# Differences of inputs moved from GpSimd to VectorE, and another order of the seven products, in a kernel of sparse attention and a gated feed-forward layer

## The chip, the cores and the metric

The kernel runs on one core of one Trainium2 chip. The metric is the device time of one execution in microseconds (us). Before the change the median of three runs is 895.81 us (894.02 to 897.63). The core has five engines that run side by side: TensorE (PE in the rows; PEld is its weight load), VectorE (DVE), ScalarE (ACT), GpSimd (POOL) and SyncE (SP), whose queue issues the DMAs.

## The reference

Eight batches of eight heads, 576 positions, 64 numbers per head. Heads 0 to 3 see the last 32 positions ("local"), heads 4 to 7 see the earlier positions with the same remainder modulo 32 ("strided"). The outputs of all heads of a position form a row x of 512 numbers; the 4608 rows then go through a feed-forward layer. All is fp32:

```python
scores = np.where(masks, q @ k.T / 8, -1e9)          # per head, mask local or strided
x = softmax(scores) @ v                              # heads side by side: 4608 x 512
h = x @ w_in                                         # 512 x 2048
g = h * (1.0 / (1.0 + np.exp(-1.702 * h)))
return g @ w_out                                     # 2048 x 512
```

## The kernel before

**Tiling.** The rows are nine groups of 512 tokens (`G`). The hidden dimension is 16 blocks of 128 (`NF`). An fp32 product is made of three products on TensorE of operands that are split in a high part (a cast on ScalarE, `high`, `split`, `high_x`, `halves`) and a low part (a subtraction, on VectorE or GpSimd): high by high, high by low, low by high. The gate is computed as (tanh(0.851 h) + 1) * h; the factor 0.5 is applied to the results.

**Attention units.** `_pairs()` lists units of attention, local and strided, in the order in which they are worked on; a unit fills a part of the x tiles of one or two groups. A unit goes through scores (PE), mask, scale and maximum (DVE, `maxima`), eight exps (ACT, `softmax`), a scaling by the inverse sums (POOL), 32x32 transposes (DVE, `transpose`, into the tile `pt_l` or `pt_s`), and the product with v (PE, `values`), whose result ACT and DVE copy into the x tiles. Units are spread over the feed-forward work of earlier groups; `TURNS` gives the step of the transposes for the first three groups.

**Plain groups.** Groups 0, 1 and 2 run as 48 steps (`steps`, loop `for s in range(2, len(steps))`): step s makes block f of the hidden layer (`ffn1`, 12 products into tile `h`), and two steps later its share of the result (`ffn2`, 12 products into the four banks `o`). During group 0 the weights are decoded and split. During group 2, `sum_up` makes for each of eight pairs of hidden blocks the sums of weights that the next stage needs: `add_up` on GpSimd (tiles `plain`, `summed`), `high_sums` on ACT, `low_sums` on DVE, and DMAs to DRAM. `SUMS` gives the steps.

**Pairs of groups.** The groups (3,4), (5,6), (7,8) are worked on two at a time (`DOUBLES`). The product with w_in for two groups by two hidden blocks is done by a scheme of Strassen and Winograd: seven products in place of eight. The operands of tokens are b11, b21 (first group, local and strided half), b12, b22 (second group) and the differences t1 = b12 - b11, t2 = b22 - t1, t3 = b22 - b12, t4 = b21 - t2 (`difference`), each with a high and a low part (`high_x`, `low_x`). The operands of weights a11, a12, a22 and the sums s1 to s4 stream from DRAM (`load_sum`). The partners are a11 with b11, s2 with t2, a12 with b21, s3 with t3, a22 with t4, s1 with t1, s4 with b22. In the trace the product of k is `ha` or `hs`, its operands `b11h`, `b11l`, `t2h`, `t2l` and so on.

A pair has eight *rounds* (`cycle`, c = 0 to 7), each with the seven products in the order of `BLOCKS`; after each product `fill(GAPS[i])` puts 4, 4, 4, 3, 3, 3, 3 products of the second layer (`o`) into PE's queue, from a list of generators (`filling`). VectorE and ScalarE combine the seven products into four hidden blocks in the tiles `spare` (s1, u2, v5, z) and `y`. Two blocks belong to the first group and are used at once. The two of the second group wait in DRAM (`gates`) until the *pass* that follows the eight rounds: 16 slots of 12 `o` products each, one hidden block per slot, loaded into `spare` and split by `halves` (ACT writes `gh`, DVE writes `gl`). In the last slots of the pass the operands of the next pair are prepared. In the tables of the engines below "opening" means the first round of a pair (c = 0).

**Order.** Each engine runs its own queue in the order in which the code issues the instructions (`InOrder` keeps it), so the places of calls in the loops set the order on every engine. Six PSUM banks are shared by the four `o`, the products of the rounds and `values`: a product of a round needs the bank of the product two before it, which is free once that one was read (by a DVE add, an ACT copy, or both).

**Tiles.** Results leave through tiles of the tag `st2` (four slots), which also holds the `y` tiles of the rounds; weights, x tiles, operands, streams and sums share 42 larger slots (`w_tile`).

## Time and profile before

| | |
|---|---|
| median of three runs | 895.81 us (894.02 to 897.63) |
| the profiled execution | 896.67 us, of which 894.9 us from the first instruction to the last |
| TensorE busy | 863.7 us (97%) |
| VectorE, ScalarE, GpSimd busy | 571.5, 426.4, 226.7 us |
| granted TensorE clock, mean | 0.992 of full speed |

Busy times overlap, since the engines run side by side. A row of the profile that shows "idle before" names the engine whose semaphore came last. All instructions have one line (L129), that of the class that keeps the order; they are told apart by the names of their tiles.

### The profile page before, as it was taken

The numbers are of one execution on the slowest core, as the hardware profiler recorded it, in microseconds if no ns is written. First come the engines' busy times: TensorE is split into PE (matmuls) and PEld (weight loads), VectorE is DVE, ScalarE is ACT, GpSimd is POOL, SyncE is SP. The second block draws the span as 40 slices with busy tenths as digits, with TensorE's granted clock in tenths as the row PEclk, the third lists the DMA queues.
The fourth block names the chain that finished last, engine by engine and source line by source line (L and its number), as shares of the span: only waits on it lengthen the run. The fifth ranks groups of instructions, "written<-read, shape, count | busy, mean of one in ns | idle before, by whom it ended". The sixth has DMA issues, their size and how long they took to land. (4 is left out here: it accounts for less than half of the span.)

```text
span 894.9 us, 15595 instructions
## 1 busy us (share of the span) xinstructions
PE 863.7 (97%) x5690; PEld 691.6 (77%) x5690; DVE 571.5 (64%) x988; ACT 426.4 (48%) x1224; POOL 226.7 (25%) x188
## 2 busy tenths in 40 slices
PE   8999999999999997999999989999999899999998
PEld 5787668888888875778887768788888688888886
DVE  4789977655676887666666686676653754444522
ACT  7798864344455455444535544553433423232421
POOL 4001001100354935232232051223220412222100
PEclk9999999999999999999999999999999999999999
DMA  9956225541263554656557525655545235454442
GB/s 282 326 228 223 100 74 177 172 162 54 79 211 117 183 166 153 208 190 191 187 183 242 177 80 159 212 175 158 161 149 196 71 112 183 146 171 146 143 124 71
DMA packets 75581, 146.40 MB, mean 164 GB/s; under 512 B 8240, under 2 KB 22960, under 8 KB 75504
## 3 DMA queue, kind: packets, MB, share of 16 engines
q1 hardware_dynamic: 75504, 145.40, 50.5%
q8 instruction: 45, 0.74, 0.3%
q14 instruction: 32, 0.26, 0.1%
HBM read 108.67 MB, written 36.70 MB: 162 GB/s over the span
## 5 line engine op out<-in xcount | busy, mean ns | idle before, releaser
L129 PE MATMUL o<-w,gh 128*128 128x512 f32 x1152 | 368.4, 396 | 0.0
L129 PEld LDWEIGHTS o<-w,gh 128*128 128x128 f32 x1152 | 216.8, 189 | 47.5 <-ACT gh L129 0.2
L129 PE MATMUL o<-w,gl 128*128 128x512 f32 x576 | 226.8, 394 | 8.0 <-DVE gl L129 8.0
L129 PEld LDWEIGHTS o<-w,gl 128*128 128x128 f32 x576 | 109.0, 189 | 33.5 <-DVE gl L129 11.1
L129 DVE SCALAR_TENSOR_TENSOR y<-tanh,y 128x512 f32<-128x512 f32 x96 | 66.5, 692 | 103.4 <-ACT tanh L129 103.4
L129 POOL TENSOR_TENSOR pr<-pr,rinv 128x432 f32<-128x432 f32 (+1 forms) x42 | 50.7, 1206 | 308.1 <-DVE rinv L129 308.1
L129 POOL TENSOR_TENSOR gl<-y,gh 128x512 fp32r<-128x512 f32 x45 | 58.1, 1291 | 226.7 <-ACT gh L129 226.7
L129 ACT ACTIVATE tanh<-y 128x512 f32<-128x512 f32 x96 | 60.7, 633 | 101.6 <-DVE y L129 95.0
L129 ACT ACTIVATE pr<-pr,nmax 128x54 f32<-128x54 f32 (+1 forms) x296 | 101.0, 346 | 0.0
L129 DVE TENSOR_TENSOR gl<-spare,gh 128x512 fp32r<-128x512 f32 x48 | 41.0, 855 | 62.2 <-ACT gh L129 61.0
L129 PE MATMUL h<-xl,w 128*128 128x512 f32 x288 | 75.9, 398 | 2.2 <-DVE w L129 0.9
L129 PE MATMUL h<-xs,w 128*128 128x512 f32 x288 | 75.2, 396 | 1.8 <-ACT xs L129 1.7
L129 ACT CAST gh<-spare 128x512 fp32r<-128x512 f32 x48 | 29.9, 622 | 79.7 <-PE o L129 79.5
L129 PEld LDWEIGHTS h<-xs,w 128*128 128x128 f32 x288 | 54.7, 191 | 14.0 <-ACT xs L129 2.1
L129 PEld LDWEIGHTS h<-xl,w 128*128 128x128 f32 x288 | 52.4, 188 | 16.6 <-DVE w L129 3.2
L129 ACT ACTIVATE g<-h 128x512 f32<-128x512 f32 x48 | 28.7, 597 | 69.8 <-PE h L129 46.0
L129 DVE STREAM_TRANSPOSE pt_l<-pr 32x256 f32<-32x256 f32 x128 | 55.6, 434 | 3.7 <-POOL pr L129 1.9
L129 DVE SCALAR_TENSOR_TENSOR g<-g,h 128x512 f32<-128x512 f32 x48 | 32.8, 684 | 39.0 <-ACT g L129 39.0
L129 ACT ACTIVATION_READ_ACCUMULATOR pr<-pr,nmax 128x1 f32 x296 | 56.4, 191 | 0.0
L129 DVE STREAM_TRANSPOSE pt_s<-pr 32x256 f32<-32x256 f32 x126 | 54.8, 435 | 2.3 <-POOL pr L129 0.5
L129 DVE TENSOR_TENSOR spare<-hs,spare 128x512 f32<-128x512 f32 x72 | 48.7, 677 | 2.1 <-PE hs L129 1.1
L129 ACT CAST gh<-g 128x512 fp32r<-128x512 f32 x48 | 29.7, 619 | 35.4 <-PE o L129 31.5
(130 smaller groups left out, 1258.3 us busy)
## 6 DMA issues: line engine op xcount, KB each, us to landing
stream<-s SPq DMA_DIRECT2D x96, 256.0 KB, 2.7
stream<-a SPq DMA_DIRECT2D x72, 256.0 KB, 2.7
gate<-y SPq DMA_DIRECT2D x48, 256.0 KB, 2.0
spare<-gate SPq DMA_DIRECT2D x48, 256.0 KB, 2.8
qk<-sqk SPq DMA_DIRECT2D x23, 452.0 KB, 4.3
qk<-lqk SPq DMA_DIRECT2D x18, 576.0 KB, 4.9
out<-out SPq DMA_DIRECT2D x36, 256.0 KB, 2.5
raw<-w_in SPq DMA_DIRECT2D x16, 512.0 KB, 7.7
```

The costliest lines, as they stand in the source:

```text
L129: ins = call(*args, **kw)
```

## The change

It has seven parts:

1. All differences of inputs and all low parts run on VectorE (`difference`, `low_x`), none on GpSimd. For the second and third pair they are spread over slots 1 to 15 of the pass before (they stood in slots 10 to 15), and the parts of t4 and b22 come in the opening.
2. In the opening the seven products come in the order `OPENING`: a11, a12, s1, s2, s3, a22, s4. v5 is made there by a copy of the product s1 and a later add of u2. For the first pair t1 is made in step 46; the others come in the opening, between its products.
3. `SUMS`: four of the eight sums of weights are made in group 1 (steps 17 to 23), four in group 2 (33 to 39).
4. `TURNS`: the units of groups 1 and 2 come one step later; in two of the windows the order of units is another one.
5. In step 16 the second layer's products come ahead of the first layer's.
6. The results of groups 2, 4, 6 and 8 go through large slots, two results to a tile.
7. In every round the tanh and the multiplication by it are issued apart, with another product's add between them; the transposes of a unit come in four portions instead of two, the exps in four portions of two.

```diff
-TURNS = ((5, 7, 9, 11, 13), (0, 2, 4, 6, 8, 10, 12, 14), (0, 2, 4, 6, 8, 10, 12))
+TURNS = ((5, 7, 9, 11, 13), (1, 3, 5, 7, 9, 11, 13, 15), (1, 3, 5, 7, 9, 11, 13))
+OPENING = ("a11", "a12", "s1", "s2", "s3", "a22", "s4")
+SUMS = (17, 19, 21, 23, 33, 35, 37, 39)
...
                     vector.transpose(out=pt[at, :, i], in_=pr[i, :, o])
-            yield
+                yield
...
-                    o = st2([P, DM], F32, f"out_{j}_{i}")
+                    if j < NN - 1 or j % 2:
+                        o = st2([P, DM], F32, f"out_{j}_{i}")
+                    else:
+                        if i % 2 == 0:
+                            two = w_tile([P, 2, DM], F32, f"out_{j}_{i}")
+                        o = two[:, i % 2]
...
-    SUMS = (0, 2, 4, 6, 8, 9, 11, 13)
...
-            at = s - (NN - 1) * NF - SUMS[c]
+            at = s - SUMS[c]
...
-        engine.tensor_tensor(out=x, in0=a, in1=b, op=ALU.subtract)
+        vector.tensor_tensor(out=x, in0=a, in1=b, op=ALU.subtract)
...
+    def convert(d, *ks):
+        for k in ks:
+            high_x(d, k)
+            low_x(d, k)
...
-        if s == -7:
-            high_x(0, "b21")
-            low_x(0, "b21", vector)
-        if s == -5:
-            high_x(0, "b11")
-            low_x(0, "b11", vector)
+        if s == -6:
+            convert(0, "b21")
+        if s == -4:
+            convert(0, "b11")
         if s == -2:
-            high_x(0, "b22")
-            low_x(0, "b22", vector)
+            difference(0, "t1")
+            convert(0, "t1")
...
-    def gate(x, y):
+    def curve(x):
         g = ffn.tile([P, G], F32, tag="g2", name="tanh", bufs=1)
         scalar.activation(g, x, AF.Tanh, scale=0.851)
-        vector.scalar_tensor_tensor(out=y, in0=g, scalar=1.0, in1=x, op0=ALU.add, op1=ALU.mult)
+        yield
+        vector.scalar_tensor_tensor(out=x, in0=g, scalar=1.0, in1=x, op0=ALU.add, op1=ALU.mult)
...
+        for i, k in enumerate(order):
+            t = ps[k] = bank(f"h{k}_{d}_{c}")
+            product(t, k)
...
+            if k == "s2":
+                add(u2, t, s1)
+                if not c:
+                    add(v5, v5, u2)
+            if k == "a12":
+                y[0] = st2([P, G], F32, f"y_{a}_{f}")
+                add(y[0], t, s1)
+                first_y = curve(y[0])
+                run(first_y, 1)
+            if k == "s3":
+                add(z, t, u2)
+                scalar.copy(out=s1, in_=t)
+                run(first_y)
+                halves((a, f), y[0], gpsimd)
...
+            if k == "s1":
+                if c:
+                    add(v5, t, u2)
+                else:
+                    scalar.copy(out=v5, in_=t)
...
+            start(i)
+            if i in (1, 2, 3, 4):
+                turned()
+            if i in (1, 2, 3, 4):
+                eased(1)
+            if i == 5:
+                eased(HU)
...
     for s in range(2, len(steps)):
+        if s == NF:
+            ffn2(s - LAG)
         ffn1(s)
...
-        if s >= LAG:
+        if s >= LAG and s != NF:
             ffn2(s - LAG)
...
-    difference(0, "t1", vector)
-    difference(0, "t2", vector)
-    difference(0, "t3", gpsimd)
+    difference(0, "t2")
     high_x(0, "t2")
-    low_x(0, "t2", vector)
-    high_x(0, "t3")
+    difference(0, "t3")
+    low_x(0, "t2")
...
         if i == 0:
             split(len(steps) - 1)
-            low_x(0, "t3", vector)
+            high_x(0, "t3")
+            difference(0, "t4")
         if i == 1:
-            difference(0, "t4", gpsimd)
-            high_x(0, "t1")
-            low_x(0, "t1", gpsimd)
+            low_x(0, "t3")
             high_x(0, "t4")
-            low_x(0, "t4", vector)
+        if i == 2:
+            low_x(0, "t4")
+            high_x(0, "b22")
+        if i == 3:
+            low_x(0, "b22")
...
-                    10: lambda: (high_x(d + 1, "b11"), low_x(d + 1, "b11", vector), difference(d + 1, "t1", gpsimd)),
...
+                    1: lambda: convert(d + 1, "b11"),
+                    2: lambda: convert(d + 1, "b21"),
+                    6: lambda: difference(d + 1, "t1"),
+                    7: lambda: convert(d + 1, "t1"),
+                    11: lambda: difference(d + 1, "t2"),
+                    12: lambda: convert(d + 1, "t2"),
+                    13: lambda: difference(d + 1, "t3"),
+                    14: lambda: convert(d + 1, "t3"),
+                    15: lambda: difference(d + 1, "t4"),
```

In the order of VectorE around the first opening, before. `xl` and `xs` are x tiles in which a difference is left, `t` holds t2, `gl_3834` is the low part of step 47's hidden block, `hs_0_0_3842` the product of s2 with t2, the second of the opening:

```order
L129 TENSOR_TENSOR xl_0_2834<-xl_0_3422,xl_0_2834 128x1024
L129 TENSOR_TENSOR t_0_3814<-xs_0_2433,xl_0_2834 128x1024
L129 TENSOR_TENSOR t2l<-t_0_3814,t2h 128x1024
L129 TENSOR_TENSOR gl_3834<-g_47_3787,gh_3833 128x512
L129 TENSOR_TENSOR t3l<-xl_0_3422,t3h 128x1024
L129 TENSOR_TENSOR spare_3751<-hs_0_0_3842,spare_3751 128x512
```

And after. `ha_0_0_3839` is the product of a12, now the second; `hs_0_0_3884` and `hs_0_0_3904` are those of s2 and s3, the fourth and the fifth:

```order
L131 TENSOR_TENSOR t_0_3811<-xs_0_2537,xl_0_2942 128x1024
L131 TENSOR_TENSOR xl_0_3500<-xs_0_2537,xl_0_3500 128x1024
L131 TENSOR_TENSOR t2l<-t_0_3811,t2h 128x1024
L131 TENSOR_TENSOR gl_3828<-g_47_3751,gh_3827 128x512
L131 TENSOR_TENSOR xs_0_1836<-xs_0_1836,t_0_3811 128x1024
L131 TENSOR_TENSOR y_0_3847<-ha_0_0_3839,spare_3725 128x512
L131 TENSOR_TENSOR t3l<-xl_0_3500,t3h 128x1024
L131 STREAM_TRANSPOSE pt_s<-pr_98 32x8x32
L131 TENSOR_TENSOR t4l<-xs_0_1836,t4h 128x1024
L131 STREAM_TRANSPOSE pt_s<-pr_98 32x8x32 x2
L131 TENSOR_TENSOR spare_3725<-hs_0_0_3884,spare_3725 128x512
L131 TENSOR_TENSOR spare_3726<-spare_3726,spare_3725 128x512
```

The difference t1 (first row before) has gone to step 46, t3 and t4 (second and fifth row after) have come from GpSimd, and between the read of a12 and that of s2 stand two low parts and three transposes.

In the order of VectorE in the pass of the first pair, slots 10 to 14, before. `gl_10` is the low part of hidden block 10 of the second group, which PE needs in the slot that follows; the low parts between are those of the second pair's operands:

```order
L129 TENSOR_TENSOR gl_10_5576<-spare_3751,gh_10_5575 128x512
L129 TENSOR_TENSOR b21l<-xs_0_2976,b21h 128x1024
L129 TENSOR_TENSOR gl_11_5597<-spare_3752,gh_11_5596 128x512
L129 TENSOR_TENSOR b22l<-xs_0_3973,b22h 128x1024
L129 TENSOR_TENSOR gl_12_5617<-spare_3752,gh_12_5616 128x512
L129 TENSOR_TENSOR t1l<-xl_0_4162,t1h 128x1024
```

And after, the same blocks:

```order
L131 TENSOR_TENSOR gl_10_5579<-spare_3725,gh_10_5578 128x512
L131 TENSOR_TENSOR t_1_5583<-xs_0_3973,xl_0_4161 128x1024
L131 TENSOR_TENSOR gl_11_5598<-spare_3726,gh_11_5597 128x512
L131 TENSOR_TENSOR t2l<-t_1_5583,t2h 128x1024
L131 TENSOR_TENSOR gl_12_5617<-spare_3726,gh_12_5616 128x512
L131 TENSOR_TENSOR xl_0_5036<-xs_0_3973,xl_0_5036 128x1024
```

There is still one operation on 1024 columns between two of these low parts; the differences, which ran on GpSimd beside them (tiles `xl`, `t`, `xs`), are now among them.

## Rows read from the trace of the kernel before

**Rows 1.** The page's slices: TensorE's busy share, tenths, 40 equal slices.

```profile
PE   8999999999999997999999989999999899999998
```

**Rows 2.** What TensorE waited for: us in total, times, longest us.

```profile
PE o L129 <- DVE gl L129: 8.0, 4, 3.1
...
PE hs L129 <- DVE spare L129: 2.6, 2, 1.4
...
PE h L129 <- ACT xs L129: 1.7, 1, 1.7
PE hs L129 <- ACT t2h L129: 1.5, 1, 1.5
PE a L129 <- DVE spare L129: 1.3, 5, 0.3
PE hs L129 <- DVE t2l L129: 1.0, 1, 1.0
...
PE hs L129 <- ACT spare L129: 0.8, 3, 0.3
PE ha L129 <- issue: 0.8, 1, 0.8
```

**Rows 3.** Two rows of TensorE's timeline in group 2: start, us, instruction [idle before].

```profile
314.46 0.96 PE L129 MATMUL a<-pt_s,v 118*64 118x108 f32 x16 [1.31 <-DVE pt_s L129]
...
328.72 0.92 PE L129 MATMUL a<-pt_l,v 96*64 96x64 f32 x24 [0.77 <-DVE pt_l L129]
```

**Rows 4.** Windows; after the five busy times: granted clock, DMA share, GB/s.

```profile
131.00:138.00 7.00, 6.64 (x38) 4.88 (x42) 5.19 (x11) 3.62 (x8) 0.91 (x1) 0.76 0.00 0
...
533.00:540.00 7.00, 6.67 (x29) 5.54 (x30) 6.20 (x7) 2.52 (x3) 0.00 (x0) 1.00 0.00 0
715.00:722.00 7.00, 6.69 (x22) 5.34 (x23) 5.64 (x7) 2.52 (x3) 0.00 (x0) 0.76 0.00 0
```

**Rows 5.** The timeline of VectorE and GpSimd in the first pair's pass.

```profile
527.10 3.42 DVE L129 TENSOR_TENSOR b22l<-xs,b22h 128x1024 fp32r<-128x1024 f32 x1
...
529.40 3.32 POOL L129 TENSOR_TENSOR xl<-xs,xl 128x1024 f32<-128x1024 f32 x1
...
530.44 2.83 DVE L129 TENSOR_TENSOR gl<-spare,gh 128x512 fp32r<-128x512 f32 x1
533.20 1.21 DVE L129 TENSOR_TENSOR t1l<-xl,t1h 128x1024 fp32r<-128x1024 f32 x1
...
534.33 0.68 DVE L129 TENSOR_TENSOR gl<-spare,gh 128x512 fp32r<-128x512 f32 x1
```

**Rows 6.** The timeline at both openings of the first two pairs.

```profile
338.43 1.17 DVE L129 TENSOR_TENSOR xl<-xl,xl 128x1024 f32<-128x1024 f32 x1
...
339.64 1.82 DVE L129 TENSOR_TENSOR t<-xs,xl 128x1024 f32<-128x1024 f32 x1
...
367.27 0.60 ACT L129 ACTIVATE out<-o 128x512 f32<-128x512 f32 x1 [4.51 <-DMA out<-out]
...
537.19 1.05 ACT L129 CAST t4h<-xs 128x1024 fp32r<-128x1024 f32 x1
...
542.90 1.77 DVE L129 STREAM_TRANSPOSE pt_l<-pr 32x256 f32<-32x256 f32 x4
```

**Rows 7.** A group of the page: ScalarE's exps, busy us, mean ns of one.

```profile
L129 ACT ACTIVATE pr<-pr,nmax 128x54 f32<-128x54 f32 (+1 forms) x296 | 101.0, 346 | 0.0
```

**Rows 8.** The chain that ended last, third pair's opening: start, us.

```profile
722.23 1.36 PE ha L129 x6
724.49 1.36 PE hs L129 x6
...
731.07 1.36 PE ha L129 x6
733.11 1.36 PE hs L129 x6
```

**Rows 9.** A window in group 2 with sums of weights in it; columns as in rows 4, busy times ahead.

```profile
280.00:300.00 20.00, 20.00 (x129) 16.07 (x128) 13.06 (x24) 11.85 (x43) 13.26 (x14) 1.00 0.39 128
```

More of the change, by code (lines that the diff above doesn't have):

```diff
@@ L527, in second @@
         gh, gl = gs.pop(g)
+        two = None
         for i in range(NT):
@@ L827, in cycle @@
         final = (d, c) == (len(DOUBLES) - 1, NF // 2 - 1)
-        def of(k):
-            ps = bank(f"h{k}_{d}_{c}")
-            product(ps, k)
-            if not final:
-                load_sum((c + 1) % (NF // 2), k)
-            return ps
+        after = p + 1 if p is not None and p + 1 < len(pairs) else None
+        order = BLOCKS if c else OPENING
+        ps, y = {}, {}
+        if p is not None:
+            turning[p] = transpose(p)
         def turned():
@@ L838, in turned @@
                 run(turning[p], 1)
-        if p is not None:
-            turning[p] = transpose(p)
-        after = p + 1 if p is not None and p + 1 < len(pairs) else None
-        ps = of("a11")
-        scalar.copy(out=s1, in_=ps)
-        start(0)
-        fill(gaps[0])
-        ps = of("s2")
-        add(u2, ps, s1)
-        turned()
-        start(1)
-        if after is not None:
-            run(soft[after], 2)
-        fill(gaps[1])
-        ps = of("a12")
-        y = st2([P, G], F32, f"y_{a}_{f}")
@@ L856, in cycle @@
-        add(y, ps, s1)
-        gate(y, y)
-        halves((a, f), y, gpsimd)
-        fill(gaps[2])
-        ps = of("s3")
-        add(z, ps, u2)
-        scalar.copy(out=s1, in_=ps)
-        turned()
-        if after is not None:
-            run(soft[after], 2)
-        fill(gaps[3])
-        ps = of("a22")
-        y3 = st2([P, G], F32, f"y_{a}_{f + 1}")
-        add(y3, ps, z)
-        gate(y3, y3)
-        if early:
-            early(0)
-        if after is not None:
-            run(soft.pop(after))
@@ L875, in cycle, with eased @@
-        start(2)
-        fill(gaps[4])
-        ps = of("s1")
-        add(v5, ps, u2)
-        if early:
-            early(1)
-        y1 = st2([P, G], F32, f"y_{b}_{f + 1}")
-        gpsimd.tensor_tensor(out=y1, in0=s1, in1=v5, op=ALU.add)
-        fill(gaps[5])
-        ps = of("s4")
-        y0 = st2([P, G], F32, f"y_{b}_{f}")
-        add(y0, ps, v5)
-        if p is not None:
-            fill(gaps[6] // 2)
-            block(p)
-            fill(gaps[6] - gaps[6] // 2)
-        else:
-            fill(gaps[6])
+        def eased(n):
+            if after is not None:
+                run(soft[after], n)
@@ new lines, in cycle @@
+        for i, k in enumerate(order):
+            t = ps[k] = bank(f"h{k}_{d}_{c}")
+            product(t, k)
+            if not final:
+                load_sum((c + 1) % (NF // 2), k)
+            if k == "a11":
+                scalar.copy(out=s1, in_=t)
[10 more added lines that the diff above has]
+                add(z, t, u2)
+                scalar.copy(out=s1, in_=t)
+                run(first_y)
+                halves((a, f), y[0], gpsimd)
+            if k == "a22":
+                y[3] = st2([P, G], F32, f"y_{a}_{f + 1}")
+                add(y[3], t, z)
+                fourth_y = curve(y[3])
+                run(fourth_y, 1)
+                if early:
+                    early(0)
+            if k == "s1":
[3 more added lines that the diff above has]
+                    scalar.copy(out=v5, in_=t)
+            if k == ("s1" if c else "a22"):
+                y[1] = st2([P, G], F32, f"y_{b}_{f + 1}")
+                gpsimd.tensor_tensor(out=y[1], in0=s1, in1=v5, op=ALU.add)
+            if k == "s4":
+                y[2] = st2([P, G], F32, f"y_{b}_{f}")
+                add(y[2], t, v5)
+            if i == 5:
+                run(fourth_y)
+                if early:
+                    early(1)
+            start(i)
[3 more added lines that the diff above has]
+                eased(1)
+            if i == 5:
+                eased(HU)
+            if i == 6 and p is not None:
+                fill(1)
+                block(p)
+                fill(GAPS[i] - 1)
+            else:
+                fill(GAPS[i])
@@ L893, in cycle @@
         filling.extend(second(a, f + i, (a, f + i)) for i in range(2))
         def rest(i):
[L896 to L902 removed]
+            last = c == NF // 2 - 1
+            if i == 0 and last:
+                halves((a, f + 1), y[3], vector)
@@ L904, in cycle @@
+            if i < 2:
+                key, x = ((f + 1, y[1]), (f, y[2]))[i]
+                run(curve(x))
+                sync.dma_start(out=gates[key], in_=x)
+            if i == 1 and not last:
+                halves((a, f + 1), y[3], gpsimd)
         return rest
     for s in range(2, len(steps)):
+        if s == NF:
+            ffn2(s - LAG)
         ffn1(s)
@@ L940, in attn_ffn @@
             if t <= s <= t + 1:
-                run(turning[p], 1)
+                run(turning[p], 2)
         for p in turn:
@@ L1034, in attn_ffn, with start @@
         if not outer:
-            def start(i):
+            def start(i, d=d, split_gate=split_gate):
                 if i == 0:
                     split_gate(NF - 1)
+                    convert(d + 1, "t4")
+                if i == 2:
+                    high_x(d + 1, "b22")
+                if i == 3:
+                    low_x(d + 1, "b22")
 def _layout(q, k, v, w_in, w_out):
```

33 lines of the change are left out of this document (10 added, 23 removed).

## The prediction

> **What bounds the kernel now.** I read the slices of the page first: TensorE is at 9 tenths or more in nearly all of them, and the reader is to see where it is not: in the first slice, the 16th (7 tenths), the 24th, the 32nd and the last [rows 1]; the three in between are the ends of group 2 and of the first two passes. The number of products stays the same, so only these dips can change. Then the list of what TensorE waited for [rows 2]. Its longest entry is 8.0 us in four waits for `gl`, the low part of a hidden block, all in the ends of the first two passes. The entries for `spare`, `t2h`, `t2l` and "issue" belong to the first opening and the round behind it. 1.7 us for `xs` stand at the start of group 1's first block in step 16. Two more waits, for transposes, stand in the last steps of group 2 [rows 3]. Last the granted clock: after three of these stops it fell to 1.2 of 2.4 GHz for a while, so that 131 to 138 us has a mean of 0.76, and 715 to 722 us too; the third stretch, 344 to 350 us, is like them. At 0.76 over 7 us, 0.24 x 7 = 1.7 us are lost [rows 4]. All of this is 8.0 + 2.6 + 1.7 + 1.5 + 1.3 + 1.0 + 0.8 + 0.8 = 17.7 us of [rows 2], 1.31 + 0.77 = 2.1 us of [rows 3], and 3 x 1.7 = 5.1 us of clock: 24.9 us.
>
> **Why PE waits in the passes.** The rows show VectorE held up beside GpSimd: the low part of b22, 1024 columns, takes 3.42 us while GpSimd computes a difference (3.32 us), and the next `gl` 2.83 us; with GpSimd idle the same two sorts take 1.21 and 0.68 us [rows 5]. A slot of a pass has 12 products, and six take 1.36 us [rows 8], so a slot lasts 2.7 us: one operation of 3.4 us and one `gl` of 2.8 us don't fit, one of 1.2 and one of 0.7 do.
>
> **The change, part by part**
>
> *Passes (differences on VectorE, one operation to a slot).* A slot then costs VectorE at most 0.68 + 1.21 = 1.9 us beside units of attention in the earlier slots only, under the 2.7 us. The 8.0 us of waits for `gl` go, and with them the fall of the clock at 715 us: 1.7 us. The eight differences of the two passes have moved, not vanished: one costs VectorE 1.17 us alone [rows 6], and the cover is TensorE's 2.7 us. Bounds: the whole 9.7 us, or nothing if the differences still hold a `gl` up; I take the whole, nearest to the row with GpSimd idle.
>
> *Opening of the first pair.* Before, it loses 2.6 + 1.5 + 1.0 + 0.8 + 0.8 = 6.7 us (two of the stops, one of 1.2 us for `spare` and 0.3 us for ScalarE's copy, are in the second round, behind results that waited 4.51 us for a slot of `st2` [rows 6]; the large slots take that wait away) and 1.7 us of clock. The new one I walk through, with T = 0 at the first product. PE's pace is 2.26 us for each of the first three products with four of the second layer behind, 2.04 us for the others [rows 8]: the products would start at 0, 2.26, 4.5, 6.8, 8.8, 10.9 and 12.9, and `values` at 14.5.
> VectorE comes out of step 47 at about T = 0.1 (an estimate: the scores end 12 products, 2.7 us, before T = 0, and mask, maximum and inverse sums fill that). Then t2, 1.82 us as it took before, or 0.65 less if GpSimd's scaling of a unit doesn't meet it [rows 6], t3 1.17, low t2 1.21, `gl` 0.68, t4 1.17, and the read of a12 (0.68, as any add of 512 columns here): done at 6.9. The fourth product needs that bank at 6.8: 0.2 us late.
> ScalarE does high t2 (1.05 [rows 6]), the copy of a11 (0.6), `gh` (0.6) and high t3 to 5.2, then waits for the read of a12 to make its tanh (7.6), then high t4 (8.6), two exps of 0.35 [rows 7] and only then the copy of the third product, s1, at about 9.9. The fifth product needs that bank at 9.1: 1.0 us late.
> VectorE goes on with low t3 (8.1), a transpose (four take 1.77 [rows 6], one 0.44), low t4 (9.9), two transposes (10.8), u2 (11.4), v5 (12.1), low b22 (13.4), a transpose, a result (14.5) and the read of s3 (15.2). The seventh product needs it at 14.2: 1.1 us late. Then the multiplication by tanh, two transposes and the read of a22 at 17.5, where `values` could start at 16.9: 0.7 us. Together 3.1 us, bounds 0 (if the queue runs ahead by as much) and 6.7 (the old loss); I take 3.1. The saving is 6.7 + 1.7 - 3.1 = 5.3 us.
>
> *Openings of the other pairs.* They had no such work; now low t4, low b22 and the extra add for v5 are on VectorE there. The same walk for the second pair (from `gl` at 3.4) gives the read of s3 at 13.1 for 12.9, and, behind eight transposes, the read of a22 at 15.4 for 14.8: about 1.0 us with the delay of the semaphores. The third pair has no attention left, and the walk gives 12.3 for 12.9: nothing. So -1.0 us; bounds 0 and -4.
>
> *Step 16.* The second layer's 12 products (2.7 us) go ahead of the block whose x is 1.7 us late; their operands were split a step earlier. The wait and its 1.7 us of clock go: 3.4 us. Bounds 0 and 3.4.
>
> *Sums and turns.* The waits of 1.31 and 0.77 us came where sums stood in odd steps beside VectorE's last half of transposes and conversions. Now every sum stands in the same position to the transposes as the first five did before, and a window with such sums shows TensorE at 20.00 of 20 us, with GpSimd at 13.26 [rows 9]. 2.1 us; bounds -5 (below) and 2.1.
>
> *Rounds.* With tanh and multiplication apart, VectorE no longer stands in front of the add that frees a bank for `values`: of the 1.3 us in five waits [rows 2] I take all. In return each add has a portion of transposes ahead (two, 0.9 us) and at most one multiplication (0.7 us). From the end of a product to the start of the second after it are at least 2 x 2.04 - 1.36 = 2.7 us, and 0.9 + 0.7 + 0.7 = 2.3 fit in.
>
> **Sum.** 9.7 + 5.3 - 1.0 + 3.4 + 2.1 + 1.3 = 20.8 us. The profiled execution took 896.67 us (its span of 894.9 and 1.8 around it): 875.9 us. It lies 0.9 us over the median, from which the same sum gives 875.0; I take 875.5.
>
> **A rule on the clock.** The rows show that the fall is no fixed price of a stop: the first pass ends with the same two waits as the second, yet 533 to 540 us has a clock of 1.00 and 715 to 722 us 0.76 [rows 4]. The Trainium skill, "TensorE: Matmul & The Clock Gate", section "What's actually happening", says that low clock is the default which activity lifts, and that the monitor runs free of the program, so that the point of the change moves from run to run. By that rule the new stops in the openings may bring a fall though they are shorter; the trace agrees in so far as like stops had unlike clocks. With all three falls back the sum would be 20.8 - 5.1 = 15.7 us.
>
> **The rivals**
>
> *1. The openings are no better than they were.* VectorE and ScalarE take the opening's work that GpSimd shared; if the first opening keeps its 6.7 + 1.7 us and the second and third lose 4 us, the gain is 20.8 - 5.3 - 3 = 12.5 us: 883.3 us from the median. For it: my walk has VectorE 5 us behind at the end of the opening, and any operation that takes the longer of its two times adds to that. Against: GpSimd is nearly empty there, so the shorter times hold.
>
> *2. The clock falls again* in three places, or the eight sums each cost as the last three did (2.1 / 3 = 0.7 us each, 5.6 in all, in place of 2.1): 15.7 or 15.2 us gained, 880 to 881 us. For it: the rows on the clock; sums now meet GpSimd's scaling of units in two groups. Against: [rows 9], and shorter stops.
>
> *3. The rounds slip, slower.* In 24 rounds every add now has transposes ahead of it, and exps stand ahead of ScalarE's copies. If a tanh or an exp is late once in a round, the waiting add holds a bank: 24 rounds at 1.2 us are 28.8 us, and 895.8 - 20.8 + 28.8 = 904 us. From 20.8 / 24 = 0.87 us per round on the kernel is slower. For it: the reserve worked out above is only 0.4 us. Against: the second of two waiting adds runs through at once, and the old order, with two waits for tanh in a row, lost only 1.3 us in all rounds.
>
> *4. It gives nothing:* rounds that slip by 0.7 to 1.0 us take the gain back.
>
> **How the numbers follow.** My forecast has 0.57, with a range of its own from 871 us (no new wait in the openings: 4.1 us less) to 879 us; rival 1 has 0.20 and rival 2 0.15. Rival 4 has 0.05 and rival 3 has 0.03. The range, 870.9 to 885 us, leaves out a gain of over 24.9 us and one of under 11. About 0.5% (4.5 us) is what a measurement of this kernel can tell from no change. Faster by more: 0.57 + 0.20 + 0.15 = 0.92; within it 0.05; slower 0.03.
>
> **What would show it.** In the profile after, the waits of PE for `gl` are under 1 us in all; every two-input operation of 1024 columns in the passes takes near 1.2 us; no stop near 130 us, and none for transposes in group 2; in the first opening three or four stops of together about 3 us, for `spare` and `y`, the longest at the fifth and the seventh product; in the second about 1 us. The forecast is wrong if TensorE's waits in rounds with c over 0 add up to more than 3 us, if `gl` still waits in the passes, or if the gain is under 12 us with the old waits gone, which would mean that products themselves take longer.

## The result, and the profile after

The changed kernel takes 868.73 us (median of four runs, 868.49 to 869.06) beside 896.72 us of the kernel before on the same chip (894.02 to 898.42): ratio 0.9691, 95% interval 0.9664 to 0.9717. The gain is 28.0 us, where 20.8 were forecast; the time lies 2.2 us under the low end of the range. The direction and most of the places were right, the size was not.

The profiled execution took 869.06 us. The page's slices, which answer to [rows 1] and to the table of engines:

```profile
span 867.0 us, 15603 instructions
PE 853.6 (98%) x5690; PEld 689.8 (80%) x5690; DVE 572.7 (66%) x999; ACT 428.9 (49%) x1227; POOL 202.4 (23%) x177
PE   8899999999999999999999999999999999999998
```

The three dips in the middle are gone. GpSimd is not empty: among its 177 instructions are 45 low parts of hidden blocks (`gl<-y,gh`), which the change left there. TensorE's idle time fell from 894.9 - 863.7 = 31.2 to 867.0 - 853.6 = 13.4 us, its busy time by 10.1 us with the same 5690 products. What TensorE waits for now, for [rows 2] (us in total, times, longest):

```profile
PE a L131 <- DVE pt_l L131: 2.6, 4, 1.2
PE a L131 <- DVE pt_s L131: 1.7, 2, 1.3
PE t L131 <- DVE zeros L131: 1.0, 1, 1.0
PE h L131 <- DVE w L131: 0.9, 3, 0.3
PE h L131 <- ACT w L131: 0.9, 1, 0.9
PE a L131 <- ACT pt_s L131: 0.6, 1, 0.6
PE hs L131 <- ACT spare L131: 0.5, 1, 0.5
PE hs L131 <- issue: 0.5, 1, 0.5
PE hs L131 <- DVE y L131: 0.2, 1, 0.2
PE o L131 <- DVE w L131: 0.2, 1, 0.2
```

`gl`, 8.0 us before, is not in the list. Below, a *stop* is idle time of TensorE ahead of a product; a short one, of 0.13 us for example, gets no idle row. Behind step 15 six stops with a row are left. One is 0.21 us near 129 us, where step 16 begins; the other five (TensorE's timeline; start, duration, instruction, idle ahead of it):

```profile
201.19 0.92 PE L131 MATMUL a<-pt_l,v 96*64 96x64 f32 x24 [0.87 <-DVE pt_l L131]
...
340.81 1.20 PE L131 MATMUL hs<-t2h,stream 128*128 128x512 f32 x4 [0.24 <-DVE y L131]
...
343.67 1.19 PE L131 MATMUL hs<-t3h,stream 128*128 128x512 f32 x4 [0.53 <-ACT spare L131]
...
348.51 1.17 PE L131 MATMUL hs<-b22h,stream 128*128 128x512 f32 x4 [0.47 <-issue]
...
350.80 0.96 PE L131 MATMUL a<-pt_s,v 118*64 118x108 f32 x16 [0.43 <-DVE pt_s L131]
```

The first is new: group 1's transposes came late. The other four are the walk's four products (fourth, fifth, seventh and `values`), 1.67 us instead of 3.1. For the fourth and the fifth the row names the read that the walk named; for the seventh it says "issue", for `values` transposes. Behind them no row shows a stop any more. VectorE in the first pair's pass, for [rows 5]:

```profile
505.69 0.69 DVE L131 TENSOR_TENSOR gl<-spare,gh 128x512 fp32r<-128x512 f32 x1 [2.09 <-ACT gh L131]
506.30 1.22 DVE L131 TENSOR_TENSOR t<-xs,xl 128x1024 f32<-128x1024 f32 x1
508.41 0.69 DVE L131 TENSOR_TENSOR gl<-spare,gh 128x512 fp32r<-128x512 f32 x1 [0.89 <-ACT gh L131]
509.36 1.23 DVE L131 TENSOR_TENSOR t2l<-t,t2h 128x1024 fp32r<-128x1024 f32 x1 [0.26 <-ACT t2h L131]
```

0.69 and 1.2 us, with idle time ahead of each `gl`, as forecast. Two windows for [rows 4] show no fall of the clock (the column behind the five busy times), and from 31 to 866 us its mean is 1.00:

```profile
131.00:138.00 7.00, 7.00 (x60) 5.57 (x60) 4.75 (x10) 3.97 (x14) 0.00 (x0) 1.00 0.25 82
345.00:352.00 7.00, 6.10 (x57) 4.51 (x59) 6.12 (x10) 3.78 (x14) 1.49 (x2) 1.00 0.25 75
```

**A table by stretches.** Where the time went is read best from start to start of the same product. The start of a kernel varies by up to 5 us between executions, so the table begins at a product of step 15 (`h<-xl` near 122 us) and ends at the last `o<-w,gl`. The marks between are the first `ha<-b11h` of a round. us:

| | step 15 to pair 1 | its opening | its rounds 2 to 7 | round 8, pass | opening 2 | rounds 2 to 7 | round 8, pass | pair 3, rounds 1 to 7 | to the end | all |
|---|---|---|---|---|---|---|---|---|---|---|
| before | 216.90 | 24.56 | 105.26 | 69.94 | 17.07 | 101.59 | 64.94 | 104.72 | 63.80 | 768.78 |
| changed | 211.54 | 19.27 | 101.45 | 64.33 | 17.13 | 100.01 | 58.50 | 104.72 | 63.69 | 740.64 |

All in all 28.14 us less. The third pair, which had no stop before, takes 104.72 us in both: products by themselves did not become faster. A second execution of the changed kernel gives 740.61, and no stretch differs by more than 0.06. Two things are less steady: the first stretch, 211.25 to 211.54 us in variants that change nothing in it, and the kernel before, whose rounds 2 to 7 took 0.7 and 0.6 us less in the execution of experiment 3 than in the table. So a tenth of a us counts in the other stretches of the changed kernel and its variants alone.

### The profile page after: what moved, and what is told of

Its sections match the earlier page's. It is cut to its first block, busy times and chain, and to the rows that moved or that the text cites. A ratio compares the mean times of both kernels' runs of the same rounds, so it can differ in the third digit from the quotient of the medians.

```text
span 867.0 us, 15603 instructions
## 1 busy us (share of the span) xinstructions
PE 853.6 (98%) x5690; PEld 689.8 (80%) x5690; DVE 572.7 (66%) x999; ACT 428.9 (49%) x1227; POOL 202.4 (23%) x177
## 4 chain that ended last, share of the span: by engine, by line
PE 86%; DVE 8%; ACT 4%; issue 1%; DMA 1%; SPq 0%; DVEq 0%; ACTq 0%
PE o L131 41%; PE hs L131 14%; PE h L131 11%; PE ha L131 11%; PE a L131 4%; PE s L131 3%; DVE raw L131 1%; DVE w L131 1%; ACT pr L131 1%; DVE pt_l L131 1%; PE t L131 1%; ACT raw L131 1%; DVE gl L131 1%; DVE pt_s L131 1%; DMA raw<-w_out 1%
## 5 line engine op out<-in xcount | busy, mean ns | idle before, releaser
L131 PE MATMUL o<-w,gl 128*128 128x512 f32 x576 | 224.4, 390 | 0.0
L131 POOL TENSOR_TENSOR gl<-y,gh 128x512 fp32r<-128x512 f32 x45 | 61.2, 1360 | 290.8 <-ACT gh L131 146.0
L131 DVE TENSOR_TENSOR gl<-spare,gh 128x512 fp32r<-128x512 f32 x48 | 33.2, 692 | 60.9 <-ACT gh L131 60.8
L131 DVE TENSOR_TENSOR y<-ha,spare 128x512 f32<-128x512 f32 x48 | 33.1, 690 | 20.7 <-PE ha L131 20.1
```

The costliest lines, as they stand in the source:

```text
L131: ins = call(*args, **kw)
```

## The experiments

Two theories stood against each other on the passes. Theory E: what held `gl` up was the engine, GpSimd beside VectorE. Rival S: it was the crowding in six slots. On the missing 7 us, theory C says that a stop costs more than its idle shows.

**1. Differences of the passes on GpSimd, in the new slots.**

```diff
-        vector.tensor_tensor(out=x, in0=a, in1=b, op=ALU.subtract)
+        (gpsimd if d else vector).tensor_tensor(out=x, in0=a, in1=b, op=ALU.subtract)
```

> Changed kernel, but the three (four with t4) differences of each of the first two passes are computed by GpSimd, in the changed kernel's slots. Theory E (what held gl up was the engine: a two-input operation of VectorE that meets a GpSimd difference takes 2.8 to 3.4 us in place of 0.7 to 1.2): gl has 1.8 us of reserve in a slot, a held one is 2.1 us late, so in each of the 8 slots with a difference TensorE stops for about 0.3 us, with the low part in the next slot held too for up to 1 us more; 4 to 9 us back, 873 to 878 us, waits for gl in the list. Rival S (what mattered is that the work is spread over more slots): no wait for gl of note, 868 to 870 us.

873.08 us (871.75 to 876.96), ratio 0.974 (0.9688 to 0.9792): 4.4 us of the gain lost, 3.4 by the stretches from step 15 on, but not by eight short stops. The first pass takes 64.37 us, as changed; the second 62.09, 3.6 more, with one stop. GpSimd and VectorE there:

```profile
655.75 2.41 POOL L131 TENSOR_TENSOR xl<-xl,xl 128x1024 f32<-128x1024 f32 x1 [5.68 <-DVE b11l L131]
...
658.24 2.72 POOL L131 TENSOR_TENSOR t<-xs,xl 128x1024 f32<-128x1024 f32 x1
...
658.63 3.41 DVE L131 TENSOR_TENSOR b21l<-xs,b21h 128x1024 fp32r<-128x1024 f32 x1
...
660.92 3.32 POOL L131 TENSOR_TENSOR xl<-xs,xl 128x1024 f32<-128x1024 f32 x1
...
661.96 5.62 DVE L131 TENSOR_TENSOR gl<-spare,gh 128x512 fp32r<-128x512 f32 x2
...
664.20 2.83 POOL L131 TENSOR_TENSOR xs<-xs,t 128x1024 f32<-128x1024 f32 x1
...
664.84 0.50 PE L131 MATMUL o<-w,gl 128*128 128x512 f32 x1 [3.07 <-DVE gl L131]
```

The slots 6, 11, 13 and 15 did not hold GpSimd back: with nothing ahead in its queue it ran all four differences in a row while TensorE was in slots 2 to 4, beside b21's low part and `gl`. In the first pass units of attention stood ahead of it; there too the low part of t2 took 3.42 us beside a difference, but no stop came of it. By the Trainium skill, "SBUF — State Buffer", section "Who interferes with whom", a VectorE instruction with both inputs in SBUF contends with one of GpSimd that reads SBUF. The trace agrees: 3.41 us beside GpSimd, 1.23 for the same operation alone.

**2. All on VectorE, in the old slots.**

```diff
-                    1: lambda: convert(d + 1, "b11"),
-                    2: lambda: convert(d + 1, "b21"),
...
+                    10: lambda: (convert(d + 1, "b11"), difference(d + 1, "t1")),
+                    11: lambda: (convert(d + 1, "b21"), difference(d + 1, "t2")),
...
+                    15: lambda: convert(d + 1, "t3", "t4"),
```

> Changed kernel, all differences and low parts on VectorE, but issued in the old slots 10 to 15 of each of the first two passes (two or three to a slot) with b22 and t4 there and not in the opening. Theory E: VectorE has 11 operations of 1.2 us and 6 gl of 0.7 us, 17.5 us, for six slots of 2.7 us (16.3 us); a slot with 0.7 + 1.2 + 1.2 us is over its 2.7 us by 0.4, within the reserve of 1.8 us; 0 to 2 us lost, less up to 1 us for openings without t4 and b22: 868 to 871 us. Rival S: the old waits for gl, 8 us with about 1.7 us of clock, come back: 876 to 879 us.

868.09 us (867.76 to 868.40), ratio 0.967 (0.9631 to 0.9709); passes of 64.33 and 58.51 us. The engine alone takes all of the loss in the passes away; the new slots add nothing to it. By experiment 1 the slots alone take 12.0 - 3.6 = 8.4 of 12.0 us. Theory E holds: without GpSimd the six crowded slots cost nothing. But S is not nothing, since with GpSimd at work the new slots (and t4 and b22 in the opening) take most of the loss away too: the old waits needed both, the meeting of the two engines and the crowding.

**3. Step 16 alone, in the kernel before.**

```diff
+        if s == NF:
+            ffn2(s - LAG)
         ffn1(s)
...
-        if s >= LAG:
+        if s >= LAG and s != NF:
```

> Kernel before with one edit: in step 16 the second layer's products of step 14 go ahead of the first layer's. The wait of 1.7 us for xs and its 1.7 us of clock go: 3.4 us by the prediction, 893.3 us from the median of 896.7. If a stop costs 0.27 us more than the idle that the trace shows (theory C): 3.7 us, 893.0. Rival: TensorE waits just behind, for the operand of step 14's products or for the read of a bank, and keeps the half: 895.

894.18 us (890.09 to 897.14), ratio 0.9972 (0.9945 to 0.9998). The spread of this kernel and of the one before is too wide for 3 us, so the table decides: 213.79 us to the first opening for 216.90, 3.1 us. The profiled execution, 890.09 us, had no fall of the clock behind any stop. Its stretches show two things. The first opening takes 24.55 us with the clock full and 24.56 with the fall: a fall ahead of a wait cost nothing, the wait just became shorter. Of the two rows, the first is from the kernel before, the second from this run:

```profile
351.55 1.19 PE L129 MATMUL hs<-t3h,stream 128*128 128x512 f32 x4 [1.38 <-DVE spare L129]
...
347.84 1.20 PE L129 MATMUL hs<-t3h,stream 128*128 128x512 f32 x4 [2.80 <-DVE spare L129]
```

From step 15 on it takes 762.79 us, 22.15 more than the changed kernel, with clock 1.00 in both; its 21 stops with a row show 19.5 us of idle, the changed kernel's six 2.75. 16.8 us of idle leave 5.4 of the 22.15 for what 15 more stops cost beyond their idle, and for stops without a row.

**4. to 6. Stops made on purpose,** in the last pass, which has none. In chosen slots some VectorE operations of 1.22 us each, into a tile that nothing reads any more, go ahead of `gl`. The edit with four of them:

```diff
+            if outer and i in (3, 6, 9, 12):
+                for _ in range(4):
...
             if 1 <= i <= NF:
                 split_gate(i - 1)
```

> Changed kernel with two more operations of VectorE (1024 columns, 1.22 us each, into a tile that nothing reads any more) ahead of gl in slots 3, 5, 7, 9, 11 and 13 of the last pass, a stretch without any stop. gl has 1.83 us of reserve, so each should stop TensorE by 2.44 - 1.83 = 0.6 us: 3.7 us of idle in the trace. Theory C (each stop costs about 0.27 us more than its idle shows, at the products beside it): 3.7 + 1.6 = 5.3 us, 874.0 us. Rival P (the excess goes with the length, 5.0 of 17.8 us): 4.7 us, 873.4. Rival N (the idle shown is all, and products became faster by themselves): 3.7 us, 872.4.

868.42 us: a miss of mine. VectorE's idle 2.0 us between two `gl` took both operations in and no stop came. The next two have more of them:

> Changed kernel with four more operations of VectorE (1024 columns, 1.22 us each, into a tile that nothing reads any more) ahead of gl in slots 3, 6, 9 and 12 of the last pass, which has no stop otherwise. Two of them fitted into VectorE's idle 2.0 us between two gl; four are 2.9 us late, and gl has about 1.8 us of reserve: four stops of about 1.1 us. The stretch from the third pair's last product to the end is compared with the changed kernel's, product by product. Theory C (a stop costs about 0.3 us more than its idle shows, whatever its length): 4 x 0.3 = 1.2 us over the idle in the trace; with 4.4 us of idle 5.6 us, 874.2 us. Rival P (the excess grows with the idle, as 5.0 to 17.8): 1.2 us too at this length. Rival N (idle is all): 873.0.

> The same with five operations in each of the four slots: stops of about 2.3 us, 9.3 us of idle. Theory C: 1.2 us over the idle, as with the shorter stops, 879.1 us. Rival P: 0.28 x 9.3 = 2.6 us over the idle, 880.5. Rival N: 877.9. Stops of 3.1 us had the clock fall behind them in some of the places of the kernel before; each fall adds 1.7 us.

874.58 us (873.98 to 875.31) with four operations, 880.89 (880.64 to 881.41) with five. TensorE at the first stop of the run with four:

```profile
825.12 0.39 PE L131 MATMUL o<-w,gl 128*128 128x512 f32 x1
825.34 0.61 PE L131 MATMUL o<-w,gh 128*128 128x512 f32 x2
827.70 0.51 PE L131 MATMUL o<-w,gl 128*128 128x512 f32 x1 [1.74 <-DVE gl L131]
828.04 0.64 PE L131 MATMUL o<-w,gh 128*128 128x512 f32 x2
828.52 0.40 PE L131 MATMUL o<-w,gl 128*128 128x512 f32 x1
```

Undisturbed, the pair at 825.34 is followed after 0.46 us, a single one after 0.22 to 0.23. Here the pair counts as busy to 825.95, 0.15 us longer than its place in the stream, and the product behind the stop holds the next up for 0.34 instead of 0.22. Both parts are counted as busy, 0.27 us, and the next pair loses 0.02.

From the third pair's eighth round to the end the run takes 69.14 us for 63.69: 5.45 us more, with 4.2 us of idle (1.74, 0.82, 0.83, 0.83). So 1.2 us are left, 0.30 for a stop: the 0.27 at once, and a little in the products that follow. With five operations it takes 11.64 us more, with 8.77 us of idle, and the clock fell behind the first stop, of 3.03 us:

```profile
826.00:832.00 6.00, 3.55 (x10) 2.85 (x11) 2.96 (x4) 0.05 (x1) 0.00 (x0) 0.78 0.30 87
832.00:838.00 6.00, 6.00 (x26) 4.86 (x26) 5.29 (x5) 1.27 (x3) 0.00 (x0) 0.94 0.16 44
```

That is 0.22 x 6 + 0.06 x 6 = 1.7 us, and 11.64 - 8.77 - 1.7 = 1.2 us are left: 0.29 for a stop again, at twice the length. Theory C holds for stops ahead of these products, of 512 columns; by its rule of 0.28 us for each us of idle rival P would have 2.5 us there, rival N none.

**7. The old order of products in the first rounds.**

```diff
-OPENING = ("a11", "a12", "s1", "s2", "s3", "a22", "s4")
+OPENING = BLOCKS
```

> Changed kernel with the old order of the seven products in the first round of each pair too (the product with t2 second, that with t1 sixth, v5 added as in other rounds); sources of VectorE's work, slots of results and the order of the conversions stay as changed. Theory O (the order is what makes the opening cheap, since t1 and b21 are ready early and t2, t3 come up to 4.5 us later): the second product waits for t2's two halves as before, 1.5 + 1.0 us, with 0.3 us more for each stop, and something at the fourth: 3 to 5 us back in the first opening, up to 1 in the second; 872 to 874.5 us. Rival L (the large slots and GpSimd's absence did it): 868 to 870 us.

867.83 us (867.33 to 867.88), ratio 0.9673 (0.9642 to 0.9704). The new order is no gain at all: with the old one the first opening takes 18.83 us for 19.27. Two stops for t2 (0.53 and 0.69 us) stand in place of four. Theory O falls: with the other parts in place, the order isn't what made the opening cheap.

**8. Results in the small slots.**

```diff
-                    if j < NN - 1 or j % 2:
+                    if True:
                         o = st2([P, DM], F32, f"out_{j}_{i}")
```

> Changed kernel with the finished results in the four slots of st2 again, which y shares. Theory B (the openings lose less than I forecast since the read of a finished result leaves its bank for the seventh product): ScalarE's out waits for a slot until a transfer has left, 4.5 us in the kernel before, so the seventh product and the copies behind out come late: 2 to 5 us back in the first opening, 0.5 to 3 in each of the next two; 871 to 877 us. Rival: the walk's two banks hold, results have no part in it, 868 to 869.5 us.

872.87 us (871.91 to 876.00), ratio 0.9739 (0.9696 to 0.9781). The size is as theory B had it, the place isn't: both openings stay (19.26 and 17.14), but the rounds behind them lose 1.39 and 2.40 us. In the second pair:

```profile
540.64 0.60 ACT L131 ACTIVATE out<-o 128x512 f32<-128x512 f32 x1 [4.08 <-DMA out<-out]
...
547.88 1.19 PE L131 MATMUL ha<-t4h,stream 128*128 128x512 f32 x4 [1.75 <-DVE y L131]
```

ScalarE stands 4.08 us before a result, and what is behind it comes late, one round on. Large slots are worth 3.6 us beside the other parts; I had priced only those of the first pair, at 1.5 us.

**9. The old sums.**

```diff
-SUMS = (17, 19, 21, 23, 33, 35, 37, 39)
+SUMS = (32, 34, 36, 38, 40, 41, 43, 45)
```

> Changed kernel with the eight sums of weights in the old steps, all in group 2; the transposes keep their new steps and portions. By the prediction the two waits of 1.31 and 0.77 us come back (2.1 us), by theory C with 0.3 us more each (2.7 us), and the new stop of 0.87 us near 201 us goes with its 0.3: 1.5 us net, 870.2 us. Rival: the waits came from the steps of the transposes, not of the sums, so none comes back and the new stop goes: 867.5 us.

868.53 us (868.09 to 870.14), ratio 0.9688 (0.9662 to 0.9714). The stretch to the first opening takes 210.41 us, 1.1 less than changed: the old waits for transposes do not come back, and the new stop near 201 us is gone. But the first opening takes 20.58, 1.3 more. So it was not the sums' place that took the waits away. What is left are the later steps and finer portions of the transposes and the other places of the conversions of b21, b11 and b22 in group 2; no run took these apart. The sums' place gives nothing in all.

**10. Tanh and multiplication joined.**

```diff
-                run(first_y, 1)
+                run(first_y)
...
-                run(fourth_y, 1)
+                run(fourth_y)
```

> Changed kernel with tanh and the multiplication by it issued one behind the other again in every round (transposes stay in their finer portions). Prediction: the five waits of values for spare come back, 1.3 us, by theory C with 5 x 0.3 more: 2.8 us, 871.5 us. Rival: the finer portions of transposes are what took these waits away, 868.5 us.

871.00 us (870.48 to 872.52), ratio 0.9715 (0.9693 to 0.9736): 2.15 us from step 15 on. 0.60 lie in the first opening, 0.94 and 0.65 in the rounds behind the openings, where the trace has a single idle row, 0.21 us. Compared product by product with the changed kernel, the rest are delays of 0.09 to 0.20 us, most of them one ahead of `values` in each round, with 0.02 us of idle. So stops too short for a row cost time too.

**11. t3 and t4 of the first opening on GpSimd.**

```diff
-        vector.tensor_tensor(out=x, in0=a, in1=b, op=ALU.subtract)
+        (gpsimd if not d and k in ("t3", "t4") else vector).tensor_tensor(
+            out=x, in0=a, in1=b, op=ALU.subtract)
```

> Changed kernel with t3 and t4 of the first opening computed by GpSimd, as before the change, in the changed places. Theory E: VectorE's low parts beside them take 3.4 in place of 1.2 us, t3 itself comes 2 us later; 2 to 5 us back between the first pair's first product and its second round, 871 to 874 us. Rival: VectorE is relieved of 2.4 us of work in a stretch where it is behind, and the opening gets better, 867 to 868.5 us.

872.52 us (870.60 to 874.89), ratio 0.973 (0.9703 to 0.9757); the first opening takes 21.54 us, 2.27 more. The operations that meet, the stop that follows, and a window behind it:

```profile
337.47 2.40 POOL L131 TENSOR_TENSOR xl<-xs,xl 128x1024 f32<-128x1024 f32 x1
337.85 3.10 DVE L131 TENSOR_TENSOR t2l<-t,t2h 128x1024 fp32r<-128x1024 f32 x1 [1.12 <-ACT t2h L131]
339.82 3.35 POOL L131 TENSOR_TENSOR xs<-xs,t 128x1024 f32<-128x1024 f32 x1
...
340.88 2.85 DVE L131 TENSOR_TENSOR gl<-g,gh 128x512 fp32r<-128x512 f32 x1
...
344.38 1.19 PE L131 MATMUL hs<-t2h,stream 128*128 128x512 f32 x4 [2.52 <-DVE y L131]
345.00:349.00 4.00, 4.00 (x12) 2.95 (x11) 3.62 (x7) 4.00 (x13) 0.00 (x0) 0.58 0.25 66
```

Two operations moved away from VectorE made two others 4.1 us longer: t2's low part and `gl` take 1.21 and 0.68 us in the changed kernel. The read of a12 behind them comes late, so the fourth product waits 2.52 us instead of 0.24. Behind this stop the clock fell (0.58 of full speed over 4 us, so 0.42 x 4 = 1.7 us lost), and of the later stops one is left, 0.30 us. Theory E holds in the opening too, but the 2.27 us are the meeting and the fall that its stop brought; what the meeting costs with the clock up was not measured.

**12. The first finished result read late.** In the first rounds, VectorE's read of bank o_0 goes behind that of the second result:

```diff
+                    late.insert(0, (i, o, ps))
+                    if i == 0 and j % 2 == 0 and NN - 1 <= j < NG - 1:
+                        yield
+                        continue
+                    for n, o, ps in late:
```

> Changed kernel; in the first rounds VectorE's read of the first finished result (bank o_0) is issued behind that of the second, one product later. Theory B (the seventh product gets the bank of o_0, a third bank that my walk did not have): it now waits for another bank; in the walk's two banks that is the end of VectorE's read of s3, 0.7 us later than its start in the first opening and 0.4 later in the second, or the late read of o_0 itself, up to 2 us later; 0.7 to 2.5 us back in the first opening, 0.7 (0.4 and 0.3 for a new stop) to 2.5 in the second: 870 to 873.5 us. Rival (the seventh product waits for something else, as the step's own issue): 868.7 us.

871.60 us (868.37 to 872.81). In the profiled execution, 870.41 us, step 15 came 1.1 us later than in the changed kernel, ahead of any edit; from there on it takes 740.96 us, 0.3 more. The wait moves as theory B says:

```profile
349.90 1.20 PE L131 MATMUL hs<-b22h,stream 128*128 128x512 f32 x4 [1.05 <-ACT spare L131]
...
532.89 1.20 PE L131 MATMUL hs<-b22h,stream 128*128 128x512 f32 x4 [0.21 <-ACT spare L131]
```

The seventh product now waits for the copy of s3, 1.05 us in the first opening and 0.21 in the second, where the walk had 1.1 and 0.2. So the changed kernel does have a third bank there, from the finished result. But the first opening takes 19.38 us for 19.27, since `values` then no longer waits, and the second 17.60 for 17.13: 0.6 us of the missing ones, less than the 1.4 that I expected at least.

**13. to 15. Towards a faster kernel.**

```diff
+OPENING = ("a11", "a12", "s2", "s3", "a22", "s1", "s4")
...
-        if NF + 2 <= s < NF + 2 + NF // 2:
-            keep(s - NF - 2)
+        if NF + 10 <= s < NF + 10 + NF // 2:
+            keep(s - NF - 10)
```

> Candidate to be faster than the changed kernel: the product with b21 second and the others in the old order in the first round of each pair (the order that only took the product with t1 to the front cost 0.4 us against the old one), and the stores of the weights' plain parts in steps 26 to 33 instead of 18 to 25, away from the sums of group 1. The opening loses its stops for t2 (0.53 and 0.69 us with 0.3 each) and the stop near 201 us (0.6 to 0.87, with 0.3) goes: 1.5 to 2.7 us from 867.8: 865.1 to 866.5 us. Rival: VectorE's read of the second product comes behind t2's conversions, and the stop only moves: 867.5 us.

871.65 us (868.81 to 872.22). The profiled execution was late by 3.5 us at step 15, ahead of any edit; from there it takes 740.00, as the old order alone (739.88). The stop near 201 us stays (0.79): the stores were not its cause. In the opening two other stops, 0.29 and 0.79 us, stand in place of those for t2.

```diff
+OPENING = BLOCKS
+SUMS = (17, 19, 21, 33, 35, 37, 39, 41)
```

> Candidate: changed kernel with the old order of products in the first rounds and with three sums in group 1 (steps 17, 19, 21) and five in group 2 (33 to 41, each second step). By the two runs before it: the order gives 0.4 us in the first opening and a little in the second; without the fourth sum of group 1 the stop of 0.6 to 0.87 us near 201 us goes with its 0.3 (the stretch from step 15 to the first opening was 1.1 us shorter with all sums in group 2), and with the last sum in step 41 the opening's t2 isn't late: 1.7 to 1.9 us in all, 866.8 to 867.0 us. Rival: a sum in step 41 makes a wait for transposes of its own, 867.8.

866.96 us (866.01 to 867.35), ratio 0.9663 (0.9634 to 0.9692): faster than both kernels. The changed kernel was run again beside it:

> The changed kernel again, beside the candidates on one chip: 868.7 us.

869.13 us (868.22 to 872.21). From step 15 on the candidate takes 738.89 for 740.61 us: the stop near 201 us is gone (210.42 to the first opening) and the opening takes 18.71. The third candidate:

```diff
+OPENING = ("a11", "a12", "s2", "s3", "a22", "s1", "s4")
...
-            high_x(0, "b22")
         if i == 3:
+            high_x(0, "b22")
+        if i == 4:
             low_x(0, "b22")
```

> Candidate: as the last, with the product with b21 second (then the old order) and the conversion of b22 one product later. Without the conversion of b22 ahead of it, ScalarE's copy for the sixth product comes 1.05 us earlier and its stop of 0.78 us (with 0.3) goes: 865.8 us. Rival: low b22 is then late for the seventh product, by up to 1 us: 867.5 us.

738.81 us from step 15 on and 868.04 (867.71 to 868.84) in all. Its stop for ScalarE's copy stays (0.84 us), so b22's conversion was not what delayed it.

## Why the prediction was off

| term | forecast | from the table | point |
|---|---|---|---|
| passes | 9.7 | 5.6 + 6.4 = 12.0 | right cause (1, 2), stops mis-sized |
| step 16 | 3.4 | 3.1 (3) | right |
| sums and turns | 2.1 | 2.2 | right size; not by the sums' place (9) |
| first opening, and rounds of pair 1 | 5.3 and part of 1.3 | 5.3 + 3.8 = 9.1 | too small |
| opening 2, and rounds of pair 2 | -1.0 and the rest of 1.3 | -0.1 + 1.6 | too small |
| all | 20.8 | 28.1 | |

**The step that failed first** is the price of a stop. The prediction took a stop to cost the idle that its row shows: "8.0 + 2.6 + ... = 17.7 us". The runs show more. Ahead of a product of 512 columns a stop costs 0.27 us on top at once, at every length from 0.8 to 3.1 us (4 to 6, and the passes of the kernel before). Ahead of the products of `values` it is mostly 0.07: in the first two rows, of the kernel before, `values` starts 0.72 us behind the product ahead of it, in the last two, of the changed kernel, 0.32, and 0.33 of the difference of 0.40 is shown as idle.

```profile
380.32 0.39 PE L129 MATMUL o<-w,gh 128*128 128x512 f32 x1
381.04 1.15 PE L129 MATMUL a<-pt_l,v 96*64 96x64 f32 x32 [0.33 <-DVE spare L129]
...
367.19 0.39 PE L131 MATMUL o<-w,gh 128*128 128x512 f32 x1
367.51 1.15 PE L131 MATMUL a<-pt_l,v 96*64 96x64 f32 x32
```

With the time from each product's start to the next one's compared in this way, the 28.1 us fall into four parts. Behind step 15 the kernel before has 21 stops with an idle row, 20.05 us, the changed one 6, 2.75: 17.3 us are idle. These 15 stops cost 3.1 us beyond it. 4.8 us are slower products in the three falls of the clock. The other 3.0 us are in stops too short for a row. The forecast had 19.8 - 4.1 = 15.7 us of idle, 5.1 of clock, and put the other two terms at nothing. So of the missing 7.3 us 6.1 are what stops cost beyond their rows, 1.6 are idle, and the clock gave 0.3 less. In the first pass the loss was 5.6 us with 4.3 us of idle, in the second 4.9 with 4.0 where the clock stayed up (3), and 1.6 more with the fall, for which the forecast had 1.7. The fall in the first opening is among the 4.8 us, but it was worth nothing, since without it the wait behind it is 1.4 us longer (3). This is also why TensorE's busy time fell by 10.1 us with the number of products the same: most of 3.1 + 4.8 + 3.0 us is shown as busy.

**The second is the walk through the openings:** 3.1 + 1.0 us of new stops were forecast, 1.7 came. Its causes were right for the fourth and the fifth product, and the fifth starts 10.06 us behind the first, where the walk had 9.1 + 1.0. For the seventh they were not: the walk had two banks for the products; the finished result's is a third (12), 0.6 us. The remaining 1.8 us I did not separate. One part is visible: TensorE comes to each further product later than the walk's pace says, by the 0.27 us that the stop before cost on top, so that it waits less. Against these 2.4 us stand 1.1 of stops that were not forecast, near 129 and 201 us; with 0.25 us of old stops that the forecast's list left out, this makes the 1.6 us of idle.

The large slots were priced too low as well: undoing them alone costs 1.4 us in the rounds of the first pair, for which I had 1.5, and 2.4 in those of the second, for which I had none (8). What made the first opening 5.3 us cheaper is shown in part only: GpSimd's two differences cost 2.3 us there (11), tanh and multiplication joined 0.6 (10), the old sums 1.3 (9), the order and the large slots nothing (7, 8); t1 in step 46 was not undone alone. The prices of single undoings overlap and don't add up.

**The rivals.** The openings did get better (rival 1 falls). No new fall of the clock came (rival 2). Rounds did not slip (rival 3): the third pair's take 104.72 us as before. Of the parts, two gave nothing and were credited in the sum or the walk: the new order of products (7) and the new place of the sums (9).

## What to carry to other kernels

A stop of TensorE costs more than the idle row says, here 0.27 us or more ahead of products of 512 columns; count stops, not only their idle, and measure from start to start of the same product. Before work is spread out to free an engine, look at which two engines slow each other down: here moving work onto the busier engine made it faster. The place of an instruction in the program holds back only an engine that has something ahead of it in its queue.

## What was not expected of the hardware

Stops of TensorE ahead of products of 512 columns had a fixed part, the same with 0.8 and with 3.1 us of idle: 0.15 us are the last product's end and 0.12 the first product's start, both shown as busy. Ahead of the smaller products of `values` it was mostly 0.07 us. The clock fell behind the first of the five-operation stops, of 3.03 us (0.78 of full speed over 6 us, 1.7 us lost), and not behind the three of 1.6 to 2.1 us that followed. It fell behind a stop of 2.52 us in experiment 11; it stayed at 1.00 behind stops of 2.8, 3.0 and 3.1 us in the execution of experiment 3, and behind that of 3.07 us in experiment 1. The part ahead of step 15, unchanged in the variants of the changed kernel, took from 120.9 to 125.6 us in their profiled executions.
